# Contiguous 4 MB transfers in a scale-and-add kernel that is bound by its DMA engines

## The chip, the core and the metric

The kernel runs on one core of one Trainium2 chip. The metric is the device time of an execution in microseconds (us). All executions below are with the granted clock at 1.00. The span of a profiled or timed execution on the core is some 1.3 us shorter than its device time.

## The reference

```python
B, S, D = 1024, 16, 512            # bf16
def reference(x, y, gamma):        # x, y: [1024, 16, 512], gamma: [512]
    return x + gamma * y
```

There are 16,384 rows of 512 elements, 16.8 MB in each of x, y and the output. Each byte goes in or out once, 50.3 MB in all.

## The kernel before

Each tensor is cut into four pieces. Partition p owns the 128 consecutive rows from 128 p, and piece c is 32 of these, so that one transfer is 128 runs of 32 KiB (32 rows of 1 KiB), 128 KiB apart in HBM.

```python
PIECES = [32, 32, 32, 32]
SP = [('x', 0), ('y', 0), ('x', 1), ('y', 1), ('y', 2), ('x', 2), ('y', 3), ('x', 3)]
ACT = [('g',), ('s', 0, 0, 2), ('s', 1, 1, 2), ('s', 2, 2, 2), ('s', 3, 3, 3)]
# ... ('s', a, b, k): store pieces a..b once add k has finished
    xv = xf.rearrange("(p n) d -> p n d", p=P)        # y and out alike
# ...
            need = X_AFTER[args[0]] if kind == "x" else args[2] if kind == "s" else -1
            if need > known:
                eng.wait_ge(s_add, need + 1)
                known = need
# ...
    for c in range(n):
        _take(s_y[c], 16, nc.vector)
        nc.vector.tensor_tensor(...y * gamma, in place..., op=MULT).then_inc(s_dve, 1)
        _take(s_x[c], 16, nc.vector)
        _take(s_dve, 1, nc.vector)
        nc.vector.tensor_tensor(...x + y, in place of y..., op=ADD).then_inc(s_add, 1)
```

SyncEngine (SP) issues the eight loads on one queue, ScalarE (ACT) the four stores on another. The first three stores wait until the third add has finished (`s_add` at 3). Adds are counted from one in the text: first to fourth.

Of the kernel before, what the change touches and what calls it, by code (L numbers as in the profile page):

```python
# [3 lines left out]


PIECES = [32, 32, 32, 32]

X_AT = [0, 32, 0, 32]
X_AFTER = [-1, -1, 0, 1]


SP = [('x', 0), ('y', 0), ('x', 1), ('y', 1), ('y', 2), ('x', 2), ('y', 3), ('x', 3)]
ACT = [('g',), ('s', 0, 0, 2), ('s', 1, 1, 2), ('s', 2, 2, 2), ('s', 3, 3, 3)]

EARLY = [('x', 0), ('y', 0), ('g',)]
MULT, ADD = mybir.AluOpType.mult, mybir.AluOpType.add


def _take(sem, n, eng):


    return eng.wait_ge(sem, n).then_inc(sem, -n)  # L22


def kernel(
    tc: tile.TileContext,
    x: bass.AP,
    y: bass.AP,
    gamma: bass.AP,
    out: bass.AP,  # L30
):



    nc = tc.nc
    P = nc.NUM_PARTITIONS
    tc.close()
    tc.compile()  # L38

    xf = x.flatten_outer_dims()  # L40
    yf = y.flatten_outer_dims()
    of = out.flatten_outer_dims()
    N, D = xf.shape
    rows = N // P
    n = len(PIECES)
    assert sum(PIECES) == rows
    starts = [sum(PIECES[:c]) for c in range(n + 1)]
    dt = xf.dtype
    xv = xf.rearrange("(p n) d -> p n d", p=P)
    yv = yf.rearrange("(p n) d -> p n d", p=P)  # L50
    ov = of.rearrange("(p n) d -> p n d", p=P)

    gamma_row = nc.alloc_sbuf_tensor("gamma_row", [1, D], dt).ap()
    ones_row = nc.alloc_sbuf_tensor("ones_row", [1, P], dt).ap()
    gamma_sb = nc.alloc_sbuf_tensor("gamma_sb", [P, D], dt).ap()
    y_sb = nc.alloc_sbuf_tensor("y_sb", [P, rows, D], dt).ap()
    x_rows = max(a + r for a, r in zip(X_AT, PIECES))
    x_sb = nc.alloc_sbuf_tensor("x_sb", [P, x_rows, D], dt).ap()
    gamma_ps = nc.alloc_psum_tensor("gamma_ps", [P, D], mybir.dt.float32).ap()

    sem = nc.alloc_semaphore
    s_gamma, s_ones, s_ps, s_dve = sem("s_gamma"), sem("s_ones"), sem("s_ps"), sem("s_dve")
    s_x = [sem(f"s_x{c}") for c in range(n)]
    s_y = [sem(f"s_y{c}") for c in range(n)]
    s_add, s_end, s_out = sem("s_add"), sem("s_end"), sem("s_out")

    def piece(a, b=None):
        return slice(starts[a], starts[(a if b is None else b) + 1])

    def x_tile(c):  # L70
        return x_sb[:, X_AT[c] : X_AT[c] + PIECES[c], :]

    early, stores = [], 0

    def ring(eng, what, known=-1):

        nonlocal stores
        for w in what:
            kind, args = w[0], w[1:]
            need = X_AFTER[args[0]] if kind == "x" else args[2] if kind == "s" else -1  # L80
            if need > known:
                eng.wait_ge(s_add, need + 1)
                known = need
            if kind == "g":
                i = eng.dma_start(out=gamma_row, in_=gamma.unsqueeze(0)).then_inc(s_gamma, 16)
            elif kind == "x":
                c = args[0]
                i = eng.dma_start(out=x_tile(c), in_=xv[:, piece(c), :]).then_inc(s_x[c], 16)
            elif kind == "y":
                c = args[0]  # L90
                i = eng.dma_start(out=y_sb[:, piece(c), :], in_=yv[:, piece(c), :])
                i.then_inc(s_y[c], 16)
            else:
                r = piece(args[0], args[1])
                i = eng.dma_start(out=ov[:, r, :], in_=y_sb[:, r, :]).then_inc(s_out, 16)
                stores += 1
            if w in EARLY:
                early.append(i.ins)

    ring(nc.sync, SP)  # L100
    ring(nc.scalar, ACT)


    nc.vector.memset(ones_row, 1.0).then_inc(s_ones, 1)  # L104
    _take(s_ones, 1, nc.tensor)
    _take(s_gamma, 16, nc.tensor)
    nc.tensor.matmul(gamma_ps, ones_row, gamma_row, start=True, stop=True).then_inc(s_ps, 1)  # L107
    _take(s_ps, 1, nc.vector)
    nc.vector.tensor_copy(out=gamma_sb, in_=gamma_ps).then_inc(s_dve, 1)  # L109
    _take(s_dve, 1, nc.vector)  # L110

    for c in range(n):
        yt = y_sb[:, piece(c), :]
        _take(s_y[c], 16, nc.vector)
        nc.vector.tensor_tensor(  # L115
            out=yt, in0=yt, in1=gamma_sb[:, None, :].to_broadcast([P, PIECES[c], D]), op=MULT
        ).then_inc(s_dve, 1)
        _take(s_x[c], 16, nc.vector)
        _take(s_dve, 1, nc.vector)
        nc.vector.tensor_tensor(out=yt, in0=x_tile(c), in1=yt, op=ADD).then_inc(s_add, 1)  # L120


    nc.scalar.sem_inc(s_end, 1)
    _take(s_end, 1, nc.sync)
    _take(s_add, n, nc.sync)
    _take(s_out, 16 * stores, nc.sync)

    main = nc.main_func.blocks[0].instructions
    names = {i.name for i in early}
    for b in nc.main_func.blocks[1:]:  # L130
        for i in [i for i in b.instructions if i.name in names]:
            b.instructions.remove(i)
    for k, i in enumerate(early):
        main.insert(1 + k, i)


# [1 line left out]
_INS = ['x', 'y', 'gamma']  # L138
_OUTS = [((1024, 16, 512), 'bfloat16')]


# [23 lines left out]
```

## Time and profile before

| | before |
|---|---|
| device time, median of the first 3 runs | 120.41 us (120.14 to 120.46) |
| profiled execution | 120.87 us, span 119.5 us |
| DMA engines, busy share (loads + stores) | 66.4 + 32.5 = 98.9% |
| VectorE, busy share | 59% |
| first store issued | 77.2 us |

The page's share of a DMA queue is the time of its packets over 16 engines times the span.

### The profile page before, as it was taken

Reading aid. Unit: us, or ns where it says so; the run is one execution under the profiler, and the core shown is the slowest. Engines: PE = TensorE matmul, PEld = TensorE weight load, DVE = VectorE, ACT = ScalarE, POOL = GpSimd, SP = SyncE. Lnnn points to the kernel's source line nnn. Section 1 sums busy time; section 2 is a strip of 40 time slices with the busy share of each in tenths; the row PEclk is TensorE's granted clock in tenths of the full one; section 3 lists DMA queues with packets and bytes.
Section 4 is the critical chain, followed back from the end, with each engine's and each line's share of the span. In section 5 each row is a group of like instructions: output and inputs, shape, how many; then the busy total and the mean of one; then the engine's idle time right before and its main releaser. Section 6 shows DMA issues by size and latency. Waiting matters only on the chain. (4 is left out here: it accounts for less than half of the span.)

```text
span 119.5 us, 84 instructions
## 1 busy us (share of the span) xinstructions
PE 0.6 (0%) x1; PEld 0.1 (0%) x1; DVE 70.2 (59%) x10; POOL 0.2 (0%) x4
## 2 busy tenths in 40 slices
PE   0100000000000000000000000000000000000000
PEld 0000000000000000000000000000000000000000
DVE  0100000699999289999999999999999600000000
POOL 0000000000000000000000000000000000000000
DMA  7989898998998989898989999898989898989995
GB/s 208 494 373 504 351 526 351 384 493 351 384 493 351 526 351 526 351 515 362 493 384 471 406 428 450 384 493 351 526 351 526 351 526 351 515 362 471 406 471 230
DMA packets 1730, 50.33 MB, mean 421 GB/s; under 512 B 193, under 2 KB 194, under 8 KB 194
## 3 DMA queue, kind: packets, MB, share of 16 engines
q1 hardware_dynamic: 1152, 33.55, 66.4%
q10 hardware_dynamic: 578, 16.78, 32.5%
HBM read 33.56 MB, written 16.78 MB: 421 GB/s over the span
## 5 line engine op out<-in xcount | busy, mean ns | idle before, releaser
L115 DVE TENSOR_TENSOR y_sb<-y_sb,gamma_sb 128x16384 bf16<-128x16384 bf16 x4 | 34.8, 8688 | 18.4 <-DVEq L22 18.4
L120 DVE TENSOR_TENSOR y_sb<-x_sb,y_sb 128x16384 bf16<-128x16384 bf16 x4 | 34.8, 8692 | 0.6
L109 DVE CAST gamma_sb<-gamma_ps 128x512 bf16<-128x512 f32 x1 | 0.7, 692 | 3.4 <-DVEq L22 3.4
L104 DVE MEMSET ones_row<- 1x128 bf16 x1 | 0.2, 165 | 2.0 <-PEq L38 2.0
L107 PE MATMUL gamma_ps<-gamma_row,ones_row 1*128 1x512 bf16 x1 | 0.6, 580 | 4.8 <-PEq L22 4.8
L107 PEld LDWEIGHTS gamma_ps<-gamma_row,ones_row 1*128 1x128 bf16 x1 | 0.1, 100 | 4.8 <-issue 4.8
L149 POOL MEMSET const-bfloat16-1.0<- 128x1 bf16 x1 | 0.1, 101 | 0.0
L149 POOL MEMSET const-uint8-127<- 128x1 uint8 x1 | 0.1, 101 | 0.0
L149 POOL MEMSET const-float32-0.0<- 128x1 f32 x1 | 0.1, 98 | 0.2 <-issue 0.2
L149 POOL MEMSET const-float32-1.0<- 128x1 f32 x1 | 0.1, 98 | 0.0
## 6 DMA issues: line engine op xcount, KB each, us to landing
x_sb<-in_x_dram SPq DMA_DIRECT2D x4, 4096.0 KB, 21.5
y_sb<-in_y_dram SPq DMA_DIRECT2D x4, 4096.0 KB, 35.4
out_dram<-y_sb ACTq DMA_DIRECT2D x4, 4096.0 KB, 23.8
gamma_row<-in_gamma_dram ACTq DMA_DIRECT2D x1, 1.0 KB
```

What stands on the lines that cost most here:

```text
L104: nc.vector.memset(ones_row, 1.0).then_inc(s_ones, 1)
L107: nc.tensor.matmul(gamma_ps, ones_row, gamma_row, start=True, stop=True).then_inc(s_ps, 1)
L109: nc.vector.tensor_copy(out=gamma_sb, in_=gamma_ps).then_inc(s_dve, 1)
L115: nc.vector.tensor_tensor(out=yt, in0=yt, in1=gamma_sb[:, None, :].to_broadcast([P, PIECES[c], D]), op=MULT).then_inc(s_dve, 1)
L120: nc.vector.tensor_tensor(out=yt, in0=x_tile(c), in1=yt, op=ADD).then_inc(s_add, 1)
L149: nc = _bacc.Bacc("TRN2", target_bir_lowering=False, num_devices=1)
```

## The change

The intent is that each transfer reads or writes one unbroken 4 MB block of HBM: a partition owns 32 consecutive rows of each quarter. The runs stay 32 KiB long; they now lie 32 KiB apart. The diff, cut to its core:

```diff
-    xv = xf.rearrange("(p n) d -> p n d", p=P)
+    xv = xf.rearrange("(c p n) d -> p c n d", p=P, n=ROWS)     # ROWS = 32; y, out alike
-ACT = [('g',), ('s', 0, 0, 2), ('s', 1, 1, 2), ('s', 2, 2, 2), ('s', 3, 3, 3)]
+ACT = [('g',), ('s', 0, 32), ('s', 32, 64), ('s', 64, 96), ('s', 96, 128)]
+DVE = [('m', 0), ('a', 0), ('m', 1), ('a', 1), ('m', 2), ('a', 2), ('go',), ('m', 3), ('a', 3)]
...
+            need = max((order[c] + 1 for c in need), default=0)     # a store: its own add
+            if kind == "s" and not went and ("go",) in DVE:
+                _take(s_go, 1, eng)
+                went = True
...
+        if kind == "go":
+            nc.vector.sem_inc(s_go, 1)
+            continue
```

So the diff holds a second thing that its title doesn't name. The stores no longer wait for the third add to finish; they wait for an increment that stands behind the third add in VectorE's program, and for their own adds.

More of the change, by code (lines that the diff above doesn't have):

```diff
@@ L6 @@
 PIECES = [32, 32, 32, 32]
-X_AT = [0, 32, 0, 32]
-X_AFTER = [-1, -1, 0, 1]
-SP = [('x', 0), ('y', 0), ('x', 1), ('y', 1), ('y', 2), ('x', 2), ('y', 3), ('x', 3)]
-ACT = [('g',), ('s', 0, 0, 2), ('s', 1, 1, 2), ('s', 2, 2, 2), ('s', 3, 3, 3)]
-EARLY = [('x', 0), ('y', 0), ('g',)]
+SP = [('x', 0, 32, 0), ('y', 0, 32), ('x', 32, 64, 32), ('y', 32, 64), ('y', 64, 96), ('x', 64, 96, 0), ('y', 96, 128), ('x', 96, 128, 32)]
+ACT = [('g',), ('s', 0, 32), ('s', 32, 64), ('s', 64, 96), ('s', 96, 128)]
+EARLY = (2, 1)
+DVE = [('m', 0), ('a', 0), ('m', 1), ('a', 1), ('m', 2), ('a', 2), ('go',), ('m', 3), ('a', 3)]
+ROWS = 32
 MULT, ADD = mybir.AluOpType.mult, mybir.AluOpType.add
@@ L48 @@
     dt = xf.dtype
-    xv = xf.rearrange("(p n) d -> p n d", p=P)
-    yv = yf.rearrange("(p n) d -> p n d", p=P)
-    ov = of.rearrange("(p n) d -> p n d", p=P)
+    xv = xf.rearrange("(c p n) d -> p c n d", p=P, n=ROWS)
+    yv = yf.rearrange("(c p n) d -> p c n d", p=P, n=ROWS)
+    ov = of.rearrange("(c p n) d -> p c n d", p=P, n=ROWS)
     gamma_row = nc.alloc_sbuf_tensor("gamma_row", [1, D], dt).ap()
@@ L56 @@
     y_sb = nc.alloc_sbuf_tensor("y_sb", [P, rows, D], dt).ap()
-    x_rows = max(a + r for a, r in zip(X_AT, PIECES))
+    x_loads = [w for w in SP + ACT if w[0] == "x"]
+    y_loads = [w for w in SP + ACT if w[0] == "y"]
+    stores = [w for w in SP + ACT if w[0] == "s"]
+    for loads in (x_loads, y_loads, stores):
+        assert sum(w[2] - w[1] for w in loads) == rows
+    x_rows = max(w[3] + w[2] - w[1] for w in x_loads)
     x_sb = nc.alloc_sbuf_tensor("x_sb", [P, x_rows, D], dt).ap()
@@ L62, with meets, pieces_of, x_at @@
     s_gamma, s_ones, s_ps, s_dve = sem("s_gamma"), sem("s_ones"), sem("s_ps"), sem("s_dve")
-    s_x = [sem(f"s_x{c}") for c in range(n)]
-    s_y = [sem(f"s_y{c}") for c in range(n)]
-    s_add, s_end, s_out = sem("s_add"), sem("s_end"), sem("s_out")
-    def piece(a, b=None):
-        return slice(starts[a], starts[(a if b is None else b) + 1])
-    def x_tile(c):
-        return x_sb[:, X_AT[c] : X_AT[c] + PIECES[c], :]
-    early, stores = [], 0
-    def ring(eng, what, known=-1):
-        nonlocal stores
-        for w in what:
-            kind, args = w[0], w[1:]
-            need = X_AFTER[args[0]] if kind == "x" else args[2] if kind == "s" else -1
+    s_load = {w: sem("s_" + "_".join(map(str, w[:2]))) for w in x_loads + y_loads}
+    s_add, s_go, s_end, s_out = sem("s_add"), sem("s_go"), sem("s_end"), sem("s_out")
+    added = [a for kind, *a in DVE if kind == "a"]
+    order = {a[0]: k for k, a in enumerate(added)}
+    def meets(a, b, c, d):
+        return a < d and c < b
+    def pieces_of(a, b):
+        return [c for c in range(n) if meets(starts[c], starts[c + 1], a, b)]
+    def x_at(row):
+        return next(w[3] + row - w[1] for w in x_loads if w[1] <= row < w[2])
+    def frees(w):
+        old = x_loads[: x_loads.index(w)]
+        old = [v for v in old if meets(v[3], v[3] + v[2] - v[1], w[3], w[3] + w[2] - w[1])]
+        return [c for v in old for c in pieces_of(v[1], v[2])]
+    early = []
+    def ring(eng, what, n_early):
+        known, went = 0, False
+        for k, w in enumerate(what):
+            kind = w[0]
+            need = frees(w) if kind == "x" else pieces_of(w[1], w[2]) if kind == "s" else []
+            need = max((order[c] + 1 for c in need), default=0)
+            if kind == "s" and not went and ("go",) in DVE:
+                _take(s_go, 1, eng)
+                went = True
             if need > known:
-                eng.wait_ge(s_add, need + 1)
+                eng.wait_ge(s_add, need)
                 known = need
@@ L86, in ring @@
             elif kind == "x":
-                c = args[0]
-                i = eng.dma_start(out=x_tile(c), in_=xv[:, piece(c), :]).then_inc(s_x[c], 16)
+                to = x_sb[:, w[3] : w[3] + w[2] - w[1], :]
+                i = eng.dma_start(out=to, in_=xv[:, w[1] // ROWS]).then_inc(s_load[w], 16)
             elif kind == "y":
-                c = args[0]
-                i = eng.dma_start(out=y_sb[:, piece(c), :], in_=yv[:, piece(c), :])
-                i.then_inc(s_y[c], 16)
-            else:
-                r = piece(args[0], args[1])
-                i = eng.dma_start(out=ov[:, r, :], in_=y_sb[:, r, :]).then_inc(s_out, 16)
-                stores += 1
-            if w in EARLY:
+                r = slice(w[1], w[2])
+                i = eng.dma_start(out=y_sb[:, r, :], in_=yv[:, w[1] // ROWS]).then_inc(s_load[w], 16)
+            else:
+                r = slice(w[1], w[2])
+                i = eng.dma_start(out=ov[:, w[1] // ROWS], in_=y_sb[:, r, :]).then_inc(s_out, 16)
+            if k < n_early:
                 early.append(i.ins)
-    ring(nc.sync, SP)
-    ring(nc.scalar, ACT)
+    ring(nc.sync, SP, EARLY[0])
+    ring(nc.scalar, ACT, EARLY[1])
     nc.vector.memset(ones_row, 1.0).then_inc(s_ones, 1)
@@ L110, with need @@
     _take(s_dve, 1, nc.vector)
-    for c in range(n):
-        yt = y_sb[:, piece(c), :]
-        _take(s_y[c], 16, nc.vector)
-        nc.vector.tensor_tensor(
-            out=yt, in0=yt, in1=gamma_sb[:, None, :].to_broadcast([P, PIECES[c], D]), op=MULT
-        ).then_inc(s_dve, 1)
-        _take(s_x[c], 16, nc.vector)
-        _take(s_dve, 1, nc.vector)
-        nc.vector.tensor_tensor(out=yt, in0=x_tile(c), in1=yt, op=ADD).then_inc(s_add, 1)
+    landed, open_mults = set(), 0
+    def need(loads, c):
+        for w in loads:
+            if w not in landed and meets(starts[c], starts[c + 1], w[1], w[2]):
+                _take(s_load[w], 16, nc.vector)
+                landed.add(w)
+    for kind, *args in DVE:
+        if kind == "go":
+            nc.vector.sem_inc(s_go, 1)
+            continue
+        c = args[0]
+        yt = y_sb[:, starts[c] : starts[c + 1], :]
+        if kind == "m":
+            need(y_loads, c)
+            g = gamma_sb[:, None, :].to_broadcast([P, PIECES[c], D])
+            nc.vector.tensor_tensor(out=yt, in0=yt, in1=g, op=MULT).then_inc(s_dve, 1)
+            open_mults += 1
+        else:
+            need(x_loads, c)
+            if open_mults:
+                _take(s_dve, open_mults, nc.vector)
+                open_mults = 0
+            at = x_at(starts[c])
+            xt = x_sb[:, at : at + PIECES[c], :]
+            nc.vector.tensor_tensor(out=yt, in0=xt, in1=yt, op=ADD).then_inc(s_add, 1)
     nc.scalar.sem_inc(s_end, 1)
@@ L125 @@
     _take(s_add, n, nc.sync)
-    _take(s_out, 16 * stores, nc.sync)
+    _take(s_out, 16 * len(stores), nc.sync)
     main = nc.main_func.blocks[0].instructions
```

## The prediction

> **What bounds the kernel now.** I read the page first for what is busy, then the DMA view for all of the span and for four stretches of it, then the timeline around the first store. The page and the DMA view:
>
> ```profile
> PE 0.6 (0%) x1; PEld 0.1 (0%) x1; DVE 70.2 (59%) x10; POOL 0.2 (0%) x4
> ...
> DMA packets 1730, 50.33 MB, mean 421 GB/s; under 512 B 193, under 2 KB 194, under 8 KB 194
> ## 3 DMA queue, kind: packets, MB, share of 16 engines
> q1 hardware_dynamic: 1152, 33.55, 66.4%
> q10 hardware_dynamic: 578, 16.78, 32.5%
> ```
>
> VectorE works 59% of the span, and the two queues together keep the 16 DMA engines busy for 66.4 + 32.5 = 98.9% of it. q1 carries the loads (33.55 MB), q10 the stores (16.78 MB). So the DMA engines are the bound from first to last, and the only things that can move the time are how long one data packet takes, and time in which the engines have none. Each transfer is 4 MB in 128 rows of 32,768 bytes, so q1 has 8 x 128 = 1024 data packets and q10 has 4 x 128 = 512; the small rest (193 under 512 B) are completions and gamma.
>
> The mean packet from these shares: loads 0.664 x 16 x 119.5 us / 1024 = 1.240 us; stores 0.325 x 16 x 119.5 / 512 = 1.214 us. The loads are slower by 0.026 us a packet, which is 0.026 x 1024 / 16 = 1.7 us of the span. Where? The DMA view cut to four stretches, in order 0 to 4, 16 to 38, 38 to 75 and 95 to 110 us:
>
> ```profile
> q1 hardware_dynamic: 32, 1.05, 79.0%
> ```
>
> ```profile
> DMA packets 319, 9.40 MB, mean 427 GB/s; under 512 B 32, under 2 KB 32, under 8 KB 32
> ...
> q1 hardware_dynamic: 319, 9.40, 102.9%
> ```
>
> ```profile
> DMA packets 545, 15.76 MB, mean 426 GB/s; under 512 B 64, under 2 KB 64, under 8 KB 64
> ...
> q1 hardware_dynamic: 545, 15.76, 98.7%
> ```
>
> ```profile
> q10 hardware_dynamic: 224, 6.29, 97.2%
> ```
>
> The columns are packets, MB and the share of 16 engines (a packet counts where it starts, hence the 102.9). Bytes over 32,768 give the data packets, and share x 16 x stretch over these the time of one: 0.790 x 16 x 4 / 32 = 1.58 us at the start, 1.029 x 16 x 22 / 287 = 1.262 us from 16 to 38, 0.987 x 16 x 37 / 481 = 1.215 us from 38 to 75, and 0.972 x 16 x 15 / 192 = 1.215 us for stores. The records of single packets agree: 1213 ns for every store and for most loads. I call 1.213 us the floor: 16 x 32,768 B / 1.213 us = 432 GB/s.
>
> Excess over the floor: start 32 x (1.58 - 1.213) / 16 = 0.73 us; 16 to 38 us 287 x (1.262 - 1.213) / 16 = 0.88 us; elsewhere next to none. The span then adds up: 1.0 us from the first issue to the first packet, 1536 / 16 = 96 packets an engine x 1.213 = 116.4, excess 1.6, completion and end 0.4, together 119.4 of 119.5 us.
>
> The timeline around the first store (start, duration, engine, line, operation):
>
> ```profile
> 59.72 0.33 SPq L88 DMA_DIRECT2D x_sb<-in_x_dram  x1
> 68.44 8.69 DVE L120 TENSOR_TENSOR y_sb<-x_sb,y_sb 128x16384 bf16<-128x16384 bf16 x1
> 77.05 8.68 DVE L115 TENSOR_TENSOR y_sb<-y_sb,gamma_sb 128x16384 bf16<-128x16384 bf16 x1
> 77.17 17.78 ACTq L95 DMA_DIRECT2D out_dram<-y_sb  x4
> 85.88 8.69 DVE L120 TENSOR_TENSOR y_sb<-x_sb,y_sb 128x16384 bf16<-128x16384 bf16 x1
> ```
>
> The reader is to see that the first store is issued 77.17 us in, just after the third add (68.44 + 8.69 = 77.13), when the loads are nearly over: by the single records the first store packet starts at 80.1 us and the last load packet ends at 80.4. So loads and stores hardly mix. The last add ends at 94.6 us, 25 us before the end. VectorE is far off the path.
>
> **What the Trainium skill says.** "DMA: Bandwidth & Descriptors", section "Where 436 GB/s comes from": 16 ports of 32 B at 850 MHz make 435 GB/s. The packets' 432 GB/s agrees to 1%. The same page, section "Latency and other measured facts", the row on HBM row pitch: copies whose rows lie 512 KiB apart ran at 207 GB/s a direction, 2 MiB apart at 164, and 214 was full rate. Here the pitch is 128 KiB before and 32 KiB after; that page has neither. The trace's 16 to 38 us stretch, 4% over the floor, could be a weak form of this, but the stretch from 38 to 75 has the same pitch and sits on the floor, so the trace supports it only in part. "Perfetto Trace Analysis", section "Contiguity and DMAs": "Contiguity only matters **within an SBUF partition line** for DMA transfers." By this the change gives nothing, and what sits on the floor agrees. "DMA: Bandwidth & Descriptors", section "Queues, rings and completion order": an engine takes turns between the queues it has work for, a packet each; the trace before hardly shows it, having so little mixing.
>
> **The change part by part.**
> 1. Addresses in HBM. A partition's rows are 32 KiB long before and after, so there are the same 1536 packets of the same size on the same engines. The instruction order is the same on every engine too. Only the distance of neighbouring rows in HBM falls from 128 to 32 KiB. The floor of 116.4 us can't move: it is the same for stores and loads, so it isn't the HBM address that sets it. What can move is the 0.88 us of the second stretch, and little of the 0.73 us of the first wave, in which all engines start at once on empty pipes. The best case is -0.9 to -1.2 us; I expect some -0.6.
> 2. The stores' gate. Before, the first store waits for the third add to finish. Now it waits for an increment that VectorE's queue holds after the third add (and each store waits for its own add). In the trace before, VectorE's sequencer takes waits while an add is still running: it consumes the semaphore of the fourth y load at 71.15 us, in the middle of the third add. So I expect the increment at 68.5 us, not 77.1, and stores 0 and 1, whose adds are done, to be issued then, 8.6 us earlier.
> 3. What the earlier stores do. At some 70 us (issue plus a lead like the first load's 1.0 us) about 80.4 - 70 = 10.5 us of loads are left. With the two queues taking turns they end near 70 + 2 x 10.5 = 91 us, so the last add runs at about 91.5 to 100 instead of 85.9 to 94.6, and the last store is issued at 100. By then the engines still have stores 1 and 2 ahead of it: all work ends at 119, and 9.7 us of it is the last store, so its turn comes at 109. Nine us of slack: no engine runs dry, and part 3 costs nothing unless mixed packets cost more than 1.213 us. I put +0.1 for that.
> The sum: 120.4 - 0.6 + 0.1 = 119.9 us.
>
> **The rivals.**
> (a) Nothing at all: the slow stretch isn't due to pitch. For: 37 us of loads with the old pitch on the floor. Then 120.3 to 120.5.
> (b) The layout costs. 16 engines now read within one 4 MB block, and could fall on the same part of the HBM; 3% on all loads would be 1024 / 16 x 0.036 = 2.3 us, so 122.7. Against: the row on pitch has small distances as the good case, and the floor leaves slack on the HBM's side for most packets.
> (c) Mixing reads and writes costs. The 20 us from 70 to 91 would have to lose 10% for 2 us: 121 to 122. The trace can't rule it out, as it has no such stretch, and the gate was there for some reason, though that could be only to let the loads go first.
> (d) The last store gets on the path because the loads are held back longer than I think. It would need 9 us more; I discount it.
> (e) Mixing gains, because a load and a store use opposite directions. A packet takes 1213 ns in both directions, which looks like an engine's own limit; then nothing is gained.
>
> **Range and chances.** From (a) 120.4 and the best case 119.2 most of the weight comes, with a tail to 121 from (b) and (c). Over 2% faster would be under 118.0, below 119.2, the floor plus what starting and ending take: 2%. Over 2% slower is over 122.8 and needs (b) or a strong (c): 5%. Predicted 119.9, range 119.1 to 121.1.
>
> **What would show it.** The load queue's share down from 66.4 towards 65.5% of a like span, and the stretch from 16 to 38 us near 1.22 us a packet: part 1 right. The first store issue at 68.5 in place of 77.2, and the last add near 91 to 100: parts 2 and 3 right; at 77 the gate fires with the add's end. Packets well over 1.213 us between 70 and 91: rival (c); over all loads: rival (b). The prediction is wrong if the time is over 121.1, or if a packet gets under 1.213 us, as the floor is then none.

## The result, and the profile after

The changed kernel takes 121.12 us (median of 6 runs, 120.91 to 121.22), against 120.39 us (6 runs, 120.14 to 120.46) for the kernel before. The ratio is 1.0064, with a 95% interval of 1.0049 to 1.0078. A ratio here is the mean time of one kernel's fast runs over that of the other's in the same rounds, so it isn't quite the ratio of the medians. By the 2% mark this is "the same"; by the interval it is 0.6% slower. It lies 0.02 us over the predicted range, and on the other side of 120.4 from the predicted 119.9.

The page after, packets, load queue and the line of the adds:

```profile
DMA packets 1730, 50.33 MB, mean 421 GB/s; under 512 B 193, under 2 KB 194, under 8 KB 194
...
q1 hardware_dynamic: 1152, 33.55, 66.1%
q10 hardware_dynamic: 578, 16.78, 32.5%
...
L157 DVE TENSOR_TENSOR y_sb<-x_sb,y_sb 128x16384 bf16<-128x16384 bf16 x4 | 34.8, 8692 | 4.6 <-DVEq L23 4.1
```

The packets are the same in number and bytes, and the loads' share went from 66.4 to 66.1%. The adds now wait 4.6 us in all where they waited 0.6: the last add waits for its x. The timeline around the first store (start, duration, engine, line, operation):

```profile
59.01 0.33 SPq L109 DMA_DIRECT2D x_sb<-in_x_dram  x1
67.73 8.69 DVE L157 TENSOR_TENSOR y_sb<-x_sb,y_sb 128x16384 bf16<-128x16384 bf16 x1
67.89 30.31 ACTq L115 DMA_DIRECT2D out_dram<-y_sb  x4
76.34 8.68 DVE L148 TENSOR_TENSOR y_sb<-y_sb,gamma_sb 128x16384 bf16<-128x16384 bf16 x1
89.14 8.69 DVE L157 TENSOR_TENSOR y_sb<-x_sb,y_sb 128x16384 bf16<-128x16384 bf16 x1 [4.11 <-DVEq L23]
```

The first store goes out at 67.89 us, 0.16 us after the third add *starts*; before, it was 77.17, after that add ended. ACT's line spans all four stores. So the increment did not wait for the add. The last add starts at 89.14 us, and the core still has work until 119.7.

The DMA view of the changed kernel from 16 to 38 us, the stretch in which the kernel before had slow loads:

```profile
q1 hardware_dynamic: 321, 9.47, 99.7%
```

9.47 MB are 289 packets, so a packet took 0.997 x 16 x 22 / 289 = 1.214 us. The slow loads are gone, and yet the run is no faster. The time came back in another place, around the first store. The DMA view from 68 to 72 us, first of the kernel before, then of the changed one:

```profile
q1 hardware_dynamic: 79, 2.06, 119.6%
```

```profile
q1 hardware_dynamic: 64, 1.57, 105.4%
```

Before, 63 load packets of 1.196 x 16 x 4 / 63 = 1.215 us; after, 48 of 1.054 x 16 x 4 / 48 = 1.405 us. In the records of single packets, each of the 16 engines has one load packet of 1.56 to 2.09 us that starts between 70.7 and 71.3 us (on four engines the next is long too, 1.36 to 1.59 us), and then its first store packet. From there on loads and stores take turns, at 1213 ns each. I call that stop the toll. Summed from the records as excess over 1213 ns, per engine:

| | start, 0 to 4 us | 16 to 38 us | around the first store |
|---|---|---|---|
| before (span 119.5) | 0.74 | 0.86 | 0.00 |
| changed (span 119.7) | 0.69 | 0.00 | 0.65 |

The rest of the difference is unevenness: the toll isn't the same on each engine, and the slowest one ends the run. Its last packet ends 0.49 us after the mean of the engines' ends in the changed kernel, and 0.19 us in the kernel before. The first column shows that the start has a like stretch: in all 14 profiles the first 4 us hold 0.51 to 0.74 us of excess in load packets, mostly in the first one of each engine. Whether the two are of one kind was not tested.

### The profile page after: what moved, and what is told of

Same layout as the page of the kernel before. It is cut to its first block, busy times and chain, and to the rows that moved or that the text cites. A ratio compares the mean times of both kernels' runs of the same rounds, so it can differ in the third digit from the quotient of the medians.

```text
span 119.7 us, 86 instructions
## 1 busy us (share of the span) xinstructions
PE 0.6 (0%) x1; PEld 0.1 (0%) x1; DVE 70.2 (59%) x10; POOL 0.2 (0%) x4
## 3 DMA queue, kind: packets, MB, share of 16 engines
q1 hardware_dynamic: 1152, 33.55, 66.1%
```

## The experiments

Two theories stood at first. A: the early stores cost the 0.7 us, the addresses nothing. B: the addresses cost, and the gate is neutral. All kernels gave correct results. Ratios are to the kernel before, run in the same rounds.

### Moving the increment, and undoing the addresses

Layout kept, increment moved behind the fourth multiply:

```diff
-DVE = [..., ('a', 2), ('go',), ('m', 3), ('a', 3)]
+DVE = [..., ('a', 2), ('m', 3), ('go',), ('a', 3)]
```

> The new addresses with the old timing of the stores: the increment stands behind the fourth multiply, so it fires at about 77.1 us instead of 67.8. Theory A (the early stores cost the 0.7 us, the addresses cost nothing or gain): 119.6 to 120.4 us, ratio to the kernel before 0.993 to 1.000, no load packet of 1.5 to 2.1 us near the first store, and the stretch from 16 to 38 us at 1.213 us a packet. Theory B (the addresses cost, the gate is neutral): about 121.1, ratio 1.006.

Measured: 121.22 us, ratio 1.0068 (1.0040 to 1.0096).

Old addresses, early gate:

```diff
-    xv = xf.rearrange("(c p n) d -> p c n d", p=P, n=ROWS)
+    xv = xf.rearrange("(p c n) d -> p c n d", p=P, n=ROWS)    # y, out alike
```

> The old addresses with the changed kernel's early gate. Theory A: 120.9 to 121.8 us, ratio 1.004 to 1.012, with one load packet of 1.5 to 2.1 us on each of the 16 engines when the stores begin and ends of the engines spread over 0.7 us. Theory B: about 120.4, ratio 1.000.

Measured: 121.03 us, ratio 1.0057 (1.0026 to 1.0087).

Both edits together, meant as the control:

> Control: old addresses and the gate at 77.1 us, but written in the changed kernel's way (an increment by VectorE, a wait on the add for each store). Both theories: as the kernel before, 120.4 us, ratio 0.998 to 1.002. If it comes at 121.1 the new way of waiting is itself the cost. Its profile also tells whether the slow loads between 16 and 38 us come again with the old addresses.

Measured: 121.08 us, ratio 1.0061 (1.0033 to 1.0088).

The first look says that nothing matters, since all three are 0.6% slower, the control too. But the edit failed. The timeline of the control:

```profile
67.45 8.69 DVE L157 TENSOR_TENSOR y_sb<-x_sb,y_sb 128x16384 bf16<-128x16384 bf16 x1
70.47 25.68 ACTq L115 DMA_DIRECT2D out_dram<-y_sb  x4
76.06 8.68 DVE L148 TENSOR_TENSOR y_sb<-y_sb,gamma_sb 128x16384 bf16<-128x16384 bf16 x1
```

The stores went at 70.47 us, still in the middle of the third add, not at 77. VectorE's sequencer had put the fourth multiply in line behind the running add as soon as its y had landed, and the increment followed at once: in the trace's records the wait for that y is taken at 70.20 us and the increment runs at 70.34. The first of the three runs shows the same, with its first store at 70.67 us. So two of these runs were not what they were meant to be, and could not acquit the gate. Old addresses with early stores (the second run) does say something: it is as slow as the changed kernel, so B falls, as the 0.6% is there without the new addresses.

One early store in place of two:

```diff
+            if w == ('s', 32, 64):
+                need = 3
```

> The changed kernel, but of the two early stores only the first goes at 67.9 us; the second waits for the third add at 76.3. Within theory A: if the cost is a single toll when stores start among loads, it stays, about 121.1 and ratio 1.006; if it grows with the number of mixed packets it shrinks to about half, 120.7 and ratio 1.003. Theory B: 121.1.

Measured: 121.09 us, ratio 1.0053 (1.0025 to 1.0082), with a toll of 0.78 us in the records. The cost in the records didn't halve, though the ratio's interval holds the 1.003 of a halved cost too. But the edit didn't halve the mixing either, so this run can't tell the two readings apart: the first store alone has eight packets for each engine, enough turns to last until the loads end. In the records 92 store packets start before the last load packet does, against 91 in the changed kernel. What speaks for a fixed toll is that the mixed packets after the stop take 1213 ns, and a comparison across runs. With 30, 60, 91 and 207 store packets started before the last load packet (the small store just before, the increment behind the multiply, the changed kernel, two starts) the toll is 0.83, 0.80, 0.65 and 0.70 us. It doesn't grow with the mixing.

### Making the stores wait for the add itself

```diff
-DVE = [..., ('a', 2), ('go',), ('m', 3), ('a', 3)]
+DVE = [..., ('a', 2), ('m', 3), ('a', 3)]
+            if kind == "s":
+                need = max(need, 3)
```

> The changed kernel without VectorE's increment; every store waits for the third add to have finished, as before. The increment moved behind the fourth multiply fired at 70.5 us all the same, so the runs so far never undid the early stores. Theory A (stores that start among the loads cost about 0.7 us, by one load packet of some 1.9 us on each engine): first store at 76 to 77 us, no such packet, 120.1 to 120.6 us, ratio 0.998 to 1.002. Theory C (something else in the new program costs 0.7, whatever the stores do): 121.1, ratio 1.006.

Measured: 120.40 us, ratio 0.9987 (0.9964 to 1.0010). The timeline now has the first store after the third add's end, and the DMA view from 68 to 72 us has 52 packets (1.70 MB) of 0.991 x 16 x 4 / 52 = 1.220 us:

```profile
67.73 8.69 DVE L159 TENSOR_TENSOR y_sb<-x_sb,y_sb 128x16384 bf16<-128x16384 bf16 x1
76.46 17.78 ACTq L117 DMA_DIRECT2D out_dram<-y_sb  x4
85.17 8.69 DVE L159 TENSOR_TENSOR y_sb<-x_sb,y_sb 128x16384 bf16<-128x16384 bf16 x1
```

```profile
q1 hardware_dynamic: 68, 1.70, 99.1%
```

This one wait takes the changed kernel from 1.0064 to 0.9987. The cost is the early stores': theory A holds. The spans agree with the sum of the parts: 119.7 - 118.9 = 0.8 us in the two profiled executions. The records give 0.65 - 0.08 = 0.57 us of toll (0.08 is what is left around the first store in this run), and the slowest engine's lag behind the mean, 0.49 - 0.27 = 0.22 us: together 0.79. These parts are of single executions. The profile of old addresses with early stores has a toll of 0.80 us and a lag of only 0.18, so how the cost splits between the two changes from one execution to the next.

The same with the old addresses, which is a control for the program's new form:

> The same with the old addresses: the kernel before, written in the new program's way. Theory A: ratio 0.998 to 1.002, and the same as the run with the new addresses to 0.3%. Theory C: 1.006. Its profile gives one more look at 16 to 38 us with the old addresses: if the 0.9 us of slow loads are the addresses' doing they come again, if not, it is one execution's chance.

Measured: 120.77 us, ratio 1.0008 (0.9980 to 1.0035). The new form costs nothing that shows. And the addresses alone, put into the kernel before:

```diff
-    xv = xf.rearrange("(p n) d -> p n d", p=P)
+    xv = xf.rearrange("(c p n) d -> p c n d", p=P, n=32)      # y, out alike
```

> The kernel before with nothing changed but the three views of the tensors: the title of the change, alone. Theory A: ratio 0.998 to 1.002 (the addresses do nothing). If the addresses took away 0.9 us of slow loads in every run: 119.5 us, ratio 0.993. If they cost: over 1.003.

Measured: 120.39 us, ratio 0.9986 (0.9962 to 1.0009). The change that the title names is worth -0.1%, with an interval that holds zero. What of the slow loads from 16 to 38 us? The DMA view of that stretch in two other runs with the old addresses, first with early stores, then with late ones:

```profile
q1 hardware_dynamic: 325, 9.60, 101.1%
```

```profile
q1 hardware_dynamic: 324, 9.57, 100.7%
```

9.60 MB are 293 packets and 9.57 MB are 292, at 1.215 and 1.214 us each: on the floor, with the old addresses. Of the four profiles with the old addresses one has the 0.86 us of slow loads, the other three have none in that stretch, and neither have any of the ten with the new addresses. So they are not a cost that the old addresses bring each time. The timed runs leave room for a little: the run above with old addresses and late stores spread from 120.21 to 121.04 us, and the kernel before, in the same rounds, from 120.18 to 121.24, but the two kernels with new addresses and late stores only from 120.24 to 120.73. Whether the new addresses make such executions rarer is open.

### What the toll belongs to

Two starts: the first store after the first add, the others after the third.

```diff
-DVE = [..., ('a', 2), ('go',), ('m', 3), ('a', 3)]
+DVE = [..., ('a', 2), ('m', 3), ('a', 3)]
+            if kind == "s" and w[1] > 0:
+                need = max(need, 3)
```

> The changed kernel with the first store sent after its own add, at 39.6 us, and the other three after the third add. The first store ends at about 63 us, loads run alone, then stores start among loads a second time. Within theory A: if each start among loads has its toll, two sets of long load packets (near 43 and near 84 us) and some 1.4 us more than the kernel before: 121.5 to 122.0, ratio 1.010 to 1.013, provided the last store still finds the engines busy. If there is one toll in a program, or the toll belongs to late loads alone: 121.1, ratio 1.006.

Measured: 121.22 us, ratio 1.0055 (1.0034 to 1.0077). The DMA view at the two starts, 40 to 44 and 80 to 84 us:

```profile
q1 hardware_dynamic: 63, 1.54, 105.7%
q10 hardware_dynamic: 1, 0.03, 1.9%
```

```profile
q1 hardware_dynamic: 54, 1.51, 87.6%
q10 hardware_dynamic: 8, 0.26, 15.2%
```

At the first start, 47 load packets (1.54 MB less completions) of 1.057 x 16 x 4 / 47 = 1.439 us; at the second, 46 of 0.876 x 16 x 4 / 46 = 1.219 us, although stores again begin among loads (8 store packets in the same view). In this program there's one toll, at the first large store; that rests on this one profile, and its six times fit it. And the time doesn't grow with some 20 us more of mixing: turns between loads and stores are free once they run.

Something could be cold at the first store, so two runs used the stores' queue beforehand. A small load on it at the start:

```diff
-ACT = [('g',), ('s', 0, 32), ...]
+ACT = [('g',), ('w',), ('s', 0, 32), ...]
+            if kind == "w":
+                eng.dma_start(out=warm, in_=xv[:, 3, 0, :]).then_inc(s_warm, 16)
```

> The changed kernel, with a small load (128 rows of 1 KB) on the stores' queue at the start, so that this queue has run on all 16 engines before the first store. In the run with two starts only the first had a toll, so something is cold at the first store. Theory T1 (the queue is cold on the engines): the long load packets near 71 us are gone and the time falls to about 120.5 (the load itself is 0.13 MB, 0.3 us at 432 GB/s), ratio 1.000 to 1.003. Theory T2 (the first writing to HBM is cold): toll stays, 121.1 to 121.4, ratio 1.006 to 1.009.

Measured: 121.28 us, ratio 1.0050 (1.0022 to 1.0077).

And a small store in its place:

```diff
+                _take(s_set, 1, eng)          # VectorE has set warm to ones
+                eng.dma_start(out=ov[:, 3, 0, :], in_=warm).then_inc(s_warm, 16)
+                _take(s_warm, 16, eng)
```

> The same with a small store (128 rows of 1 KB of ones, into rows of out that the last store writes over) in place of the load. T1 and T2: no long load packets near 71 us, about 120.5, ratio 1.000 to 1.003. If they stay here too, nothing is cold: T3, the size or the length of the first store among loads matters, and the cause of the toll is open; 121.1 to 121.4.

Measured: 121.16 us, ratio 1.0045 (1.0016 to 1.0073). The times alone are unclear, as the kernel before had a median of 120.65 in these rounds. The DMA view from 68 to 72 us decides, first of the run with the small load, then of the one with the small store:

```profile
q1 hardware_dynamic: 66, 1.64, 109.0%
```

```profile
q1 hardware_dynamic: 62, 1.51, 104.6%
```

1.64 MB are 50 packets of 1.395 us, and 1.51 MB are 46 of 1.455 us. The toll is there, 0.59 and 0.71 us in the records. So neither the queue's first use nor a first small write to HBM explains it.

The same small store at 59 us, and no longer at 2.8 us:

```diff
+                eng.wait_ge(s_add, 2)
```

> The small store of the run before last (128 rows of 1 KB), sent after the second add, at about 59 us, some 9 us ahead of the first large store, instead of at 2 us. Theory T4 (the path of the stores is cold after a long idle time): the long load packets move to about 62 us, or are gone, and none are left near 71 us; 120.7 to 121.2. Theory T3 (the toll belongs to the first large store among loads, whatever went before): 16 or more long load packets near 71 us once more, and 121.1 to 121.5, ratio 1.004 to 1.008. If it is T3 the mechanism of the toll stays open.

Measured: 121.44 us, ratio 1.0083 (1.0049 to 1.0117). The small store lands 14 us after it was issued, as it takes turns with loads of 32 KiB, and holds the first large store back to 73.4 us. The toll stays with the large store. The DMA view from 74 to 78 us, 33 load packets (1.08 MB) of 0.832 x 16 x 4 / 33 = 1.61 us:

```profile
q1 hardware_dynamic: 33, 1.08, 83.2%
q10 hardware_dynamic: 3, 0.10, 5.7%
```

Last, all stores behind the loads in the loads' own queue, with the early gate:

```diff
-ACT = [('g',), ('s', 0, 32), ('s', 32, 64), ('s', 64, 96), ('s', 96, 128)]
+ACT = [('g',)]
-SP = [..., ('x', 96, 128, 32)]
+SP = [..., ('x', 96, 128, 32), ('s', 0, 32), ('s', 32, 64), ('s', 64, 96), ('s', 96, 128)]
```

> The changed kernel, with the stores issued by SyncEngine, on the loads' queue, behind the last load; the gate is as early as in the changed kernel (67.8 us). If the toll comes from two queues taking turns on an engine, it is gone, since in one queue the stores come after all loads: 120.2 to 120.6 us, ratio 0.998 to 1.001, first store packet at about 79 to 80 us. If issuing early is what costs, 121.1.

Measured: 120.75 us, ratio 1.0010 (0.9982 to 1.0037). Issued as early (67.92 us), the stores don't overtake loads, and the time is near that of the kernel before. But the toll is not quite gone. The DMA view from 76 to 80 us:

```profile
q1 hardware_dynamic: 57, 1.51, 99.2%
```

46 load packets (1.51 MB) of 0.992 x 16 x 4 / 46 = 1.380 us. In the records the last load packet before the first store is stretched on all 16 engines, to 1.37 to 1.99 us, 0.47 us of excess in the mean. So taking turns isn't the cause either; a load in front of the first large store can pay without it. In the four profiles whose first store packet follows the last load from another queue, the excess of all packets from 66 to 84 us is 0.00 (before), 0.05 (before, with new addresses), 0.08 (new addresses, new form) and 0.26 us (old addresses, new form). What makes the stop is open. What is shown is when it comes: once, at the first large store, 0.6 to 0.8 us where that store starts among loads from another queue, 0.0 to 0.3 where it starts as they run out, and 0.5 where it stands behind them in their own queue.

No run beats the kernel before clearly; the best ratios, 0.9986 and 0.9987, have intervals that hold 1.

## Why the prediction was wrong

- **The bound** was right: the 16 DMA engines without a pause, a floor of 1.213 us a packet for loads and stores, in every run. No packet was clearly under it.
- **Part 1, the addresses (-0.6 us)** was wrong. Alone they give a ratio of 0.9986, some -0.2 us, with zero inside the interval. The step that failed is taking the 0.88 us of one execution for the kernel's property, and subtracting it from the median of other executions. Its own time, 120.87 us against a median of 120.41, said that it held about 0.5 us which most runs don't have. Rival (a), nothing from the addresses, was the right one. The sign named for part 1, about 1.22 us a packet from 16 to 38 us, came true with 1.214 and still proved nothing, since three profiles with the old addresses show the same.
- **Part 2, the gate at 68.5 us** was right: 67.89, from the observation that VectorE's sequencer goes on during an add.
- **Part 3, the earlier stores (+0.1 us)** had the course right: the turns (80 load and 78 store packets start between 72 and 84 us), the last add at 89.1 to 97.8 us where 91.5 to 100 was predicted, and the last store off the path. The lead was off: the first store packet came 4.7 us after its issue and not some 1 us, so fewer loads were left. That cost no time. The price was the term that failed: +0.1 us was put down, and a toll of 0.65 us came, with unevenness that adds some 0.2. Rival (c) had mixing cost something, and its 121 to 122 us holds the result, but that is luck: it put the cost on every packet over 20 us, while mixed packets run at 1.213 us and the cost is the one stop at the first store.
- **Rivals (b), (d) and (e)** fall: in the changed kernel all load packets but those near the start and the first store are on the floor, the last store waits for nothing, and turns gain nothing.

With the terms as measured, 120.4 - 0.2 + 0.65 + 0.2 = 121.05, where 121.12 was measured. The -0.2 in this sum can't be told from zero, and the last two are of one execution, so a fit this close is partly luck.

## What to carry to other kernels

Before a slow stretch in one profile is counted as a gain, compare that execution's time with the median of the runs: a surplus there belongs to the execution. An increment placed behind an instruction in an engine's program can fire while that instruction still runs, here 0.03 us after its start; where its end is meant, let the instruction itself do the increment. In this kernel, bound by its DMA engines, a rearrangement of addresses that kept the runs of 32 KiB gave -0.1%, which can't be told from nothing, and letting the first large store start while loads were still running cost some 0.6%.

## What the Trainium skill lacked or had wrong

- "DMA: Bandwidth & Descriptors", section "Latency and other measured facts": the row on HBM row pitch has 512 KiB and more. Here 128 KiB and 32 KiB gave the same within 0.4% (ratio 0.9986, 0.9962 to 1.0009).
- No page tells of a stop at the first large store: 0.6 to 0.8 us an engine in the mean when a 4 MB store starts among 4 MB loads, once in this program, not removed by small transfers on the same queue beforehand.
- "DMA: Bandwidth & Descriptors", section "Queues, rings and completion order" has engines take turns a packet at a time. The records agree, with one row of 32 KiB at a turn. It could add what this does to a small transfer: 128 rows of 1 KB took 14 us to land beside loads whose packets are 32 KiB.
